# Row maxima between expert matmuls: listed places and a seventh bank, an output addition on two other engines, and an earlier overflow loop

## Chip, core and metric

The kernel runs on one core of a Trainium2 chip. Its engines work side by side: TensorE (PE in the profile; its weight loads are PEld), VectorE (DVE), ScalarE (ACT), GpSimd (POOL) and SyncE (SP, which issues most DMAs). The metric is the time of one execution in device microseconds.

## The reference, cut to what matters

```python
x = A_x                                             # 1 x 2048 x 448
g = sigmoid((x * gate_w).sum(-1, keepdims=True))
# A: full attention, 16 heads of 28
q, k, v = split_heads(x @ wqkv)
p = softmax(q @ k.T * 28 ** -0.5)
a = merge_heads(p @ v) @ wo
# B: mixture of 8 experts, each token goes to its top 2
logits = x @ w_gate
gates = softmax(top2(logits))
for e in range(8):
    h = silu(x @ w1[e]) @ w2[e]                     # 448 -> 1792 -> 448
    b += (gate of e for this token, else 0) * h
out = g * a + (1 - g) * b
```

All inputs are float32.

## The kernel before

There are three stages. The first (to about 134 us in the profiled execution) makes v, the gate and expert logits, the routing, and the queries and keys, which it stores in DRAM as a high and a low half. The second (134 to 957 us) computes the experts, each on its own gathered rows. The third is the attention: scores, exponential, values, projection, and the sum with the experts' rows.

The softmax of the attention needs, for each query and head, the maximum of its scores before the third stage starts. These maxima are computed in the second stage, between the experts' matmuls, from the high halves alone. `max_stream` is a generator over 1024 cells: group of four heads `g`, query tile `qt` of 128, key block `kc` of 512, head `j` in the group. A cell is one matmul with 28 rows (line 101); the four heads of a group lie on four row groups of the array. One step takes six cells into the six banks of the PSUM tile `pm`, and one VectorE instruction reduces the six (line 116). After the 16 cells of a query tile a small reduction folds them into `mg` (line 123), and after four query tiles `store_max` transposes `mg` on TensorE (line 133) into a new `pm` tile, copies it (line 135) and stores it in `m_d` (line 136). `pm` has one buffer of six banks; the two other banks of the eight are the accumulators `acc0` and `acc1`, which the experts use in turn.

An expert has two halves of seven hidden tiles (`NH`). In a half the first layer comes first: for each hidden tile two column halves of 288 tokens, 11 matmuls each (line 797), since inputs and weights are split in a high and a low part. ScalarE makes the hidden activations, GpSimd their low parts. Then the second layer takes five token tiles in the order 4, 0, 1, 2, 3: the tail tile 4 of 64 tokens (line 835) and four tiles of 128 tokens with 21 matmuls each (line 841). In the first half ScalarE copies the sums to `ysb` (line 849); in the second half VectorE adds `ysb` to the accumulator (line 859) and SP stores the sum in `ys_d` (line 861). In the second half of all experts but the last, `turn_x` also transposes the next expert's rows in the tiles, into the accumulator that is idle (line 696), and ScalarE copies them out twice (lines 699 and 700).

Where a step of the maxima goes is set by a running count. `worked(ns)` is called after every matmul of the experts with its assumed time, and once 3350 ns are owed, the next step of `max_stream` is issued:

```python
MAX_EVERY, STORE_NS = 3350, 1000
U_NS, Y_NS, YT_NS = 131, 206, 452
def worked(ns, fit=True):
    owed[0] += ns
    if fit and owed[0] >= MAX_EVERY:
        owed[0] = MAX_EVERY - STORE_NS if next(ms, 1) == 2 else 0
```

In a second half `fit` holds only for the first four matmuls of a token tile. The order on TensorE, VectorE, ScalarE and GpSimd is the order of the program; SP's issues are placed by the scheduler.

Tokens beyond 576 per expert go to overflow tiles, which `spilled` computes in a loop with a number of turns known only at run time (line 730; its inner loop goes over pairs of hidden tiles). It stands in the last token tile of the last expert, behind the fifth hidden tile; what is left of the maxima is issued right before it (`maxes(1 << 20)`).

Of the kernel before, what the change touches and what calls it, by code (L numbers as in the profile page):

```python
# [8 lines left out]
F32 = mybir.dt.float32  # L9
# [3 lines left out]
AF = mybir.ActivationFunctionType  # L13
ALU = mybir.AluOpType
AX = mybir.AxisListType
# [6 lines left out]
MAX_EVERY, STORE_NS = 3350, 1000  # L22
U_NS, Y_NS, YT_NS = 131, 206, 452
# [12 lines left out]
NF = FF // 128  # L36
# [13 lines left out]
def tile_gated_mha_moe(ctx: ExitStack, tc: tile.TileContext, x, wqkv, wo, wgate, w1, w2, gw, out):  # L50
# [38 lines left out]

    def max_stream():  # L90
        cells = [(g, qt, kc, j) for g in range(NG) for qt in range(NT) for kc in range(4) for j in range(4)]
        kh = {(0, c): load_khg(0, c) for c in range(4)}
        qgs = {(0, 0): load_qg(0, 0)}
        mgs, mps = {}, {}
        yield 0
        for b in range(0, len(cells), 6):
            step = cells[b:b + 6]
            pm = pmx.tile([128, 6, 512], F32, name="pm")
            for n, (g, qt, kc, j) in enumerate(step):
                rw = slice(32 * j, 32 * j + DH)  # L100
                nc.tensor.matmul(pm[:, n], qgs[g, qt // 4][rw, (qt % 4) * 128:(qt % 4 + 1) * 128],  # L101
                                 kh[g, kc][rw], start=True, stop=True)
# [10 lines left out]
            if b // 48 not in mps:  # L113
                mps[b // 48] = mxp.tile([128, 48], F32, name="mp")
            o = b % 48
            nc.vector.tensor_reduce(mps[b // 48][:, o:o + len(step)], pm[:, 0:len(step)], axis=AX.X, op=ALU.max)  # L116
            for n, (g, qt, kc, j) in enumerate(step):
                if kc == 3 and j == 3:
                    if qt % 4 == 0:
                        mgs[g, qt // 4] = mxp.tile([128, 4, 4], F32, name="mg")  # L120
                    mg = mgs[g, qt // 4]
                    part = mps[b // 48][:, o + n - 15:o + n + 1].rearrange("p (k j) -> p j k", j=4)
# [3 lines left out]
            yield 1  # L126
            if flush:
                store_max(*flush.pop())
                yield 2

    def store_max(g, qc, mg):
        pmt = pmx.tile([128, 6, 512], F32, name="pm")
        nc.tensor.transpose(pmt[0:16, 0, 0:128], mg.rearrange("p j t -> p (j t)"), ident)
        mr = mxp.tile([16, 128], F32R, name="mr")
        nc.vector.tensor_copy(mr, pmt[0:16, 0, 0:128])
        nc.sync.dma_start(m_d[4 * g + qc].rearrange("h (t q) -> (h t) q", q=128), mr.bitcast(F32))
        done.append((g, qc))

    flush = []
    done = []  # L140
    ms = max_stream()

    def maxes(n):
        for _ in range(n):
            next(ms, None)

    def need_max(g, qc):
        while (g, qc) not in done:
            next(ms, None)
# [18 lines left out]
    owed = [0]  # L168
# [53 lines left out]
    with ExitStack() as pa:  # L222
# [365 lines left out]
        maxes(1)  # L588
# [60 lines left out]
    with ExitStack() as pb:  # L649
# [39 lines left out]

        xf = sb.tile([128, 4, 512], F32, name="xf", bufs=1)  # L690
# [35 lines left out]
        def spilled():  # L726
# [3 lines left out]
            with tc.For_i(0, n_spill, 1) as it:  # L730
# [15 lines left out]
                with tc.For_i(0, NF // 2, 1) as c:  # L746
                    w1t_ = pe.tile([128, 4, 256], F32, name="w1r", bufs=3)
                    cs = ds(c * 256, 256)
                    nc.sync.dma_start(w1t_[:, 0:3], w1f[ds(ev * D, 384), cs].rearrange("(b p) n -> p b n", p=128))
                    nc.sync.dma_start(w1t_[0:64, 3], w1f[ds(ev * D + 384, 64), cs])  # L750
                    pu = pmx.tile([128, 6, 512], F32, name="pm")
                    for f in range(2):
                        w2t_ = sb.tile([128, D], F32, name="w2r", bufs=9)
                        nc.sync.dma_start(w2t_, w2f[ds(ev * FF + c * 256 + f * 128, 128)])
                        for b in range(4):
                            kk = 128 if b < 3 else 64
                            nc.tensor.matmul(pu[:, f, 0:128], w1t_[:kk, b, f * 128:(f + 1) * 128], xT[:kk, b],
                                             start=b == 0, stop=b == 3)
                        hT = sb.tile([128, 512], F32, name="hf32", bufs=3)[:, 0:128]
                        nc.scalar.activation(hT, pu[:, f, 0:128], AF.Silu)  # L760
                        nc.tensor.matmul(pu[:, 2, 0:D], hT, w2t_, start=f == 0, stop=f == 1)
                    nc.vector.tensor_tensor(yo, pu[:, 2, 0:D], yo, op=ALU.add)
                nc.sync.dma_start(ys_d[ds(it * 128 + NMAIN, 128)], yo)

        for e in range(E):
# [6 lines left out]
            for hf in range(2):  # L772
                hs = []
                lag = None
                for f in range(NH):
# [17 lines left out]
                    for c in range(2):  # L793
                        cs = slice(c * HC, (c + 1) * HC)
                        pu = accumulator()
                        for i, (a, b) in enumerate(mms):
                            nc.tensor.matmul(pu[:, 0:HC], a, b[:, cs], start=i == 0, stop=i == len(mms) - 1)  # L797
                            worked(U_NS)
# [22 lines left out]
                for n_k, k in enumerate((4, 0, 1, 2, 3)):  # L821
# [4 lines left out]
                    i = 0  # L826
                    for f in range(NH):
                        hh, hl, ht = hs[f]
                        w2h, w2l, w2r = w2t[base + f]
                        if (e, hf, n_k, f) == (E - 1, 1, 4, NH // 2 + 1):  # L830
                            maxes(1 << 20)
                            spilled()
                        if k == 4:
                            for c in range(2):
                                nc.tensor.matmul(py[64 * c:64 * c + n, 0:w], ht, w2r[:, c * w:(c + 1) * w],
                                                 start=f == 0, stop=f == NH - 1)
                            worked(YT_NS, hf == 0 or f == 0)
                            fetch_w2(base + f + 9)
                            continue
                        for a, b in ((hh, w2h), (hh, w2l), (hl, w2h)):  # L840
                            nc.tensor.matmul(py[:n, 0:w], a[:, cs], b, start=i == 0, stop=i == 3 * NH - 1)  # L841
                            i += 1
                            worked(Y_NS, hf == 0 or i < 5)
# [12 lines left out]
                    else:  # L856
                        r0 = e * CPAD + k * 128
                        yo = sb.tile([128, D], F32, name="yo")
                        nc.vector.tensor_tensor(yo[:, 0:w], py[:, 0:w], ysb[k][:, 0:w], op=ALU.add)
# [190 lines left out]
```

## Time and profile before

| | |
|---|---|
| time, median of 3 runs | 1495.57 us (1494.75 to 1496.4) |
| time of the profiled execution | 1493.23 us |
| its span in the profile | 1491.4 us |
| TensorE busy | 1473.6 us, 99% |
| VectorE, ScalarE, GpSimd busy | 806.7, 882.3, 613.8 us |
| expert stage | about 134 to 957 us |
| attention, without the projection | about 957 to 1445 us |

A row of the timeline gives start, duration, engine, line, operation, the tile written and the tiles read, and in brackets the idle time before it with what ended it. A stage row gives for each engine its busy time (and instructions), then the granted TensorE clock as a share of full speed, the DMA share and GB/s. A row of the table of waits gives the total, how often, and the longest. Queues carry a q (PEldq, SPq).

### The profile page before, as it was taken

To read this page: it belongs to the slowest core of one execution; us is meant where nothing else is said; L and a number is where in the kernel's file an instruction comes from. 1 tells how busy PE (TensorE), PEld (TensorE's weight loads), DVE (VectorE), ACT (ScalarE), POOL (GpSimd) and SP (SyncE) were. 2 spreads that over 40 slices of the span, in tenths; PEclk is the share of its full clock that TensorE was granted. 3 is DMA by queue.
4 is the path that set the end of the run, shared out by engine and by line. 5 is a ranking of instruction groups with operands and counts; after the bars stand their busy time and mean duration, and the time that the engine had idled before them with its cause. 6 is when DMAs were issued, how large, how long until landed. Compare 5 with 4: busy or idle time off the path is not lost. (4 is left out here: it accounts for less than half of the span.)

```text
span 1491.4 us, 28369 instructions
## 1 busy us (share of the span) xinstructions
PE 1473.6 (99%) x11380; PEld 984.5 (66%) x11380; DVE 806.7 (54%) x672; ACT 882.3 (59%) x1539; POOL 613.8 (41%) x667
## 2 busy tenths in 40 slices
PE   8999999999999999999999999899999999999998
PEld 7878788788888887887888888533333333333348
DVE  4644777777768777767777777311122111123245
ACT  5324354344334433543443344399999999999981
POOL 2123575476457546754764565111113111214330
PEclk9999999999999999999999999999999999999999
DMA  9777631343233143313422410300221121143212
GB/s 322 259 250 233 177 96 55 106 123 96 76 120 114 42 124 120 96 54 107 126 84 73 120 60 1 92 21 21 68 66 52 54 66 34 29 112 107 71 37 103
DMA packets 107958, 147.97 MB, mean 99 GB/s; under 512 B 17356, under 2 KB 83308, under 8 KB 107824
## 3 DMA queue, kind: packets, MB, share of 16 engines
q1 hardware_dynamic: 98192, 124.90, 27.0%
q0 software_dynamic: 9344, 20.78, 4.8%
q8 instruction: 90, 1.47, 0.4%
q10 hardware_dynamic: 288, 0.46, 0.1%
q14 instruction: 44, 0.36, 0.1%
HBM read 108.56 MB, written 37.51 MB: 98 GB/s over the span
## 5 line engine op out<-in xcount | busy, mean ns | idle before, releaser
L116 DVE TENSOR_REDUCE mp<-pm 128x6 f32<-128x3072 f32 x171 | 573.1, 3351 | 141.7 <-PE pm L101 141.2
L966 ACT ACTIVATE P<-ps 128x1536 f32<-128x1536 f32 x256 | 370.7, 1448 | 0.0
L975 PE MATMUL po<-P,V 128*32 128x512 f32 x2048 | 273.7, 606 | 0.0
L797 PE MATMUL acc<-xeh,w1l 128*128 128x288 f32 x880 | 258.2, 300 | 0.0
L797 PE MATMUL acc<-xeh,w1h 128*128 128x288 f32 x880 | 257.3, 299 | 0.0
L714 POOL TENSOR_TENSOR w2l<-w2r,w2h 128x448 fp32r<-128x448 f32 x112 | 128.9, 1151 | 235.8 <-ACT w2h L708 204.9
L963 PEld LDWEIGHTS ps<-Q,Kh 29*128 29x128 f32 (+1 forms) x2048 | 79.4, 184 | 216.2 <-ACT P L965 215.7
L799 ACT ACTIVATE hh<-acc 128x288 fp32r<-128x288 f32 x224 | 92.1, 411 | 178.4 <-PE acc L797 178.4
L797 PE MATMUL acc<-xel,w1h 128*128 128x288 f32 x660 | 197.1, 299 | 0.0
L963 PE MATMUL ps<-Q,Kh 29*128 29x512 f32 (+1 forms) x2048 | 192.6, 446 | 1.6 <-ACT P L965 1.5
L930 POOL DMA_DIRECT2D sum_d<-osb x64 | 31.9, 509 | 353.6 <-DVE osb L979 353.6
L797 PEld LDWEIGHTS acc<-xeh,w1l 128*128 128x128 f32 x880 | 166.1, 189 | 14.4 <-issue 14.2
L841 PE MATMUL acc<-w2h,hh 128*128 128x448 f32 x448 | 171.4, 383 | 2.3 <-DMA Kh<-neg_d 2.3
L797 PEld LDWEIGHTS acc<-xeh,w1h 128*128 128x128 f32 x880 | 165.9, 189 | 11.2 <-issue 11.0
L841 PE MATMUL acc<-w2l,hh 128*128 128x448 f32 x448 | 169.3, 378 | 0.0
L841 PE MATMUL acc<-w2h,hl 128*128 128x448 f32 x448 | 165.9, 370 | 0.0
L979 DVE COPY osb<-po 128x512 f32<-128x512 f32 x16 | 11.1, 691 | 283.2 <-PE po L975 283.2
L965 ACT ACTIVATE P<-ps 128x512 f32<-128x512 f32 x256 | 153.0, 598 | 7.0 <-PE ps L963 6.2
L679 POOL TENSOR_TENSOR w1l<-w1r,w1h 128x512 fp32r<-128x512 f32 (+1 forms) x88 | 137.8, 1566 | 19.2 <-ACT w1h L673 6.9
L723 POOL TENSOR_TENSOR hl<-hf,hh 128x512 fp32r<-128x512 f32 x112 | 143.2, 1286 | 0.0
L797 PEld LDWEIGHTS acc<-xel,w1h 128*128 128x128 f32 x660 | 124.7, 189 | 7.9 <-issue 7.7
L101 PE MATMUL pm<-khg,qg 28*128 28x512 f32 x1024 | 124.9, 460 | 1.1 <-DVE mp L116 1.0
(179 smaller groups left out, 1855.3 us busy)
## 6 DMA issues: line engine op xcount, KB each, us to landing
w2r<-in_B_w_dram SPq DMA_DIRECT2D x112, 224.0 KB
w1r<-in_B_w_dram SPq DMA_DIRECT2D x56, 384.0 KB
w1r<-in_B_w_dram SPq DMA_DIRECT2D x112, 64.0 KB
qkh_d<-hi SPq DMA_DIRECT2D x28, 256.0 KB
qkl_d<-lo SPq DMA_DIRECT2D x28, 256.0 KB
ys_d<-yo SPq DMA_DIRECT2D x32, 224.0 KB
ys_d<-zf SPq DMA_DIRECT2D x24, 224.0 KB
v_d<-v_s SPq DMA_DIRECT2D x16, 256.0 KB
```

What stands on the lines that cost most here:

```text
L101: nc.tensor.matmul(pm[:, n], qgs[g, qt // 4][rw, (qt % 4) * 128:(qt % 4 + 1) * 128], kh[g, kc][rw], start=True, stop=True)
L116: nc.vector.tensor_reduce(mps[b // 48][:, o:o + len(step)], pm[:, 0:len(step)], axis=AX.X, op=ALU.max)
L679: nc.gpsimd.tensor_tensor(l[:, :, half], r[:, :, half], h[:, :, half].bitcast(F32), op=ALU.subtract)
L714: nc.gpsimd.tensor_tensor(w2l, w2r, w2h.bitcast(F32), op=ALU.subtract)
L723: nc.gpsimd.tensor_tensor(hl, hf32, hh[:, 0:512].bitcast(F32), op=ALU.subtract)
L797: nc.tensor.matmul(pu[:, 0:HC], a, b[:, cs], start=i == 0, stop=i == len(mms) - 1)
L799: nc.scalar.activation(hh[:, cs], pu[:, 0:HC], AF.Silu)
L841: nc.tensor.matmul(py[:n, 0:w], a[:, cs], b, start=i == 0, stop=i == 3 * NH - 1)
L963: nc.tensor.matmul(p3[:, j - 1] if j else p1, k[rw, ks], qs[u][rw, c], start=i == 0, stop=i == 2)
L965: nc.scalar.activation(P[:, 0], p1, AF.Exp, scale=SCALE)
L966: nc.scalar.activation(P[:, 1:4], p3, AF.Exp, scale=SCALE)
L975: nc.tensor.matmul(po[32 * j:32 * j + 32], v[:, kt % 8, 32 * j:32 * j + 32], P[:, j], start=kt == 0, stop=kt == NT - 1)
```

## The change

- The planner's count is gone. `w1_due` lists the places in a half's first layer where a step goes: five, or six in the second halves of the last four experts (`six`). In the second layer one step goes to the start of the tail tile (with `six`: behind its fourth hidden tile) and one to each of the four other token tiles, at the fifth or the twelfth matmul (`free_at`).
- In those four tiles a step takes seven cells: the first goes to the bank of the accumulator that is idle just then (`other_accumulator`), and has a reduction of its own; the six others go to `pm` as before. Exceptions are the second half's first tile of 128 tokens where it transposes in two places (`two`).
- `store_max` no longer takes a `pm` tile: it transposes into the idle accumulator's bank, at such a place, in a step's stead; the step follows `STORE_NS` = 600 ns later. The maxima lie in one ring of 256 columns.
- The second half's sum is made by a ScalarE copy out of the accumulator and a GpSimd addition, no longer by VectorE.
- The loop over overflow tokens stands in the tile before the last, behind its third hidden tile, and its inner loop takes one hidden tile a turn instead of two. All maxima have been issued by then.

The diff, cut:

```diff
-MAX_EVERY, STORE_NS = 3350, 1000
+STORE_NS = 600
...
-        for b in range(0, len(cells), 6):
-            step = cells[b:b + 6]
+        mp = mxp.tile([128, 256], F32, name="mp", bufs=1)
+        while b < len(cells):
+            more = len(spare)
+            step = cells[b:b + 6 + more]
             pm = pmx.tile([128, 6, 512], F32, name="pm")
+            banks = spare[:] + [pm[:, n] for n in range(len(step) - more)]
...
-                nc.tensor.matmul(pm[:, n], qgs[g, qt // 4][rw, ...],
+                nc.tensor.matmul(banks[n], qgs[g, qt // 4][rw, ...],
                                  kh[g, kc][rw], start=True, stop=True)
...
+            if more:
+                nc.vector.tensor_reduce(mp[:, o:o + 1], banks[0], axis=AX.X, op=ALU.max)
...
-    def store_max(g, qc, mg):
-        pmt = pmx.tile([128, 6, 512], F32, name="pm")
-        nc.tensor.transpose(pmt[0:16, 0, 0:128], mg.rearrange("p j t -> p (j t)"), ident)
+    def store_max(g, qc, mg, bank):
+        nc.tensor.transpose(bank[0:16, 0:128], mg.rearrange("p j t -> p (j t)"), ident)
...
-    def worked(ns, fit=True):
-        owed[0] += ns
-        if fit and owed[0] >= MAX_EVERY:
-            owed[0] = MAX_EVERY - STORE_NS if next(ms, 1) == 2 else 0
+    def worked(ns, due=False, bank=None):
+        hold[0] = max(0, hold[0] - ns)
+        want[0] += due
+        if want[0] and not hold[0]:
+            if flush and bank:
+                store_max(*flush.pop(0), bank())
+                hold[0] = STORE_NS
+                return
+            if bank:
+                spare.append(bank())
+            next(ms, None)
+            want[0] -= 1
+            spare.clear()
...
+        def other_accumulator():
+            return ps.tile([128, 512], F32, name=f"acc{turn[0] ^ 1}")
...
-                with tc.For_i(0, NF // 2, 1) as c:
+                with tc.For_i(0, NF, 1) as f:
...
+        NM = 11
+        w1_due = [(18, 46, 73, 100, 128), (7, 33, 59, 85, 111, 137)]
...
+                six = hf == 1 and e >= E - 4
...
-                            worked(U_NS)
+                            worked(U_NS, 2 * NM * f + c * NM + i in w1_due[six])
...
+                    turns = hf == 1 and e + 1 < E
+                    two = turns and n_k == 1
+                    free_at = 12 if n_k == 1 and six or turns and not two else 5
+                    if k == 4:
+                        worked(0, not six)
...
-                        if (e, hf, n_k, f) == (E - 1, 1, 4, NH // 2 + 1):
-                            maxes(1 << 20)
+                        if (e, hf, n_k, f) == (E - 1, 1, 3, 3):
+                            assert not flush and next(ms, 0) == 0
                             spilled()
...
-                            worked(YT_NS, hf == 0 or f == 0)
+                            worked(YT_NS, six and f == 3)
...
-                            worked(Y_NS, hf == 0 or i < 5)
+                            worked(Y_NS, i == free_at, other_accumulator if free_at <= i < 17 and not two else None)
...
-                        nc.vector.tensor_tensor(yo[:, 0:w], py[:, 0:w], ysb[k][:, 0:w], op=ALU.add)
+                        nc.scalar.activation(yo[:, 0:w], py[:, 0:w], AF.Copy)
+                        nc.gpsimd.tensor_tensor(yo[:, 0:w], yo[:, 0:w], ysb[k][:, 0:w], op=ALU.add)
```

More of the change, by code (lines that the diff above doesn't have):

```diff
@@ L140, in tile_gated_mha_moe @@
     done = []
+    spare = []
     ms = max_stream()
-    def maxes(n):
-        for _ in range(n):
-            next(ms, None)
     def need_max(g, qc):
-        while (g, qc) not in done:
-            next(ms, None)
+        assert (g, qc) in done
     def tail_twice(xt):
@@ L586, in first_x @@
                 x_tile(xgs[k], k, lambda: ps.tile([128, 4, 128], F32, name="pt"), *xe)
-        maxes(1)
+        next(ms)
         xgs = [gather(0, k) for k in range(5)]
```

59 lines of the change are left out of this document (30 added, 29 removed).

## The prediction

> **What bounds the kernel now.** I read the page's first part, then the busy times by stage, then who waited for whom, and last the rows of TensorE in order of time. The first fence is the page (busy time; two groups: count, busy us, mean ns, idle before), then one stretch of the expert stage, then two rows of the table of waits.
>
> ```profile
> PE 1473.6 (99%) x11380; PEld 984.5 (66%) x11380; DVE 806.7 (54%) x672; ACT 882.3 (59%) x1539; POOL 613.8 (41%) x667
> L116 DVE TENSOR_REDUCE mp<-pm 128x6 f32<-128x3072 f32 x171 | 573.1, 3351 | 141.7 <-PE pm L101 141.2
> L101 PE MATMUL pm<-khg,qg 28*128 28x512 f32 x1024 | 124.9, 460 | 1.1 <-DVE mp L116 1.0
> ```
> ```profile
> 200.00:300.00 100.00, 99.74 (x664) 81.60 (x663) 75.33 (x36) 40.74 (x111) 59.44 (x53) 1.00 0.31 95
> ```
> ```profile
> PE acc L841 <- DMA Kh<-neg_d: 2.3, 1, 2.3
> PE pm L101 <- DVE mp L116: 1.0, 4, 0.3
> ```
>
> TensorE is busy 99.74 of 100 us in the expert stage, ScalarE 40.74, GpSimd 59.44, VectorE 75.33. Nearly nothing holds TensorE up: four short waits for the maxima, and one of 2.3 us at the loop over overflow tokens. So the time of this stage is the number of TensorE instructions times what each costs, and only fewer or cheaper TensorE steps can shorten it. The max matmuls come as 171 bursts among the experts' matmuls. What is a burst worth? These are TensorE's rows in order of time (start, duration, instruction):
>
> ```profile
> 204.09 0.29 PE L797 MATMUL acc<-xel,w1h 128*128 128x288 f32 x1
> 204.22 0.29 PE L797 MATMUL acc<-xeh,w1l 128*128 128x288 f32 x1
> 204.44 0.73 PE L101 MATMUL pm<-khg,qg 28*128 28x512 f32 x6
> 205.11 0.40 PE L797 MATMUL acc<-xeh,w1h 128*128 128x288 f32 x1
> 205.34 0.30 PE L797 MATMUL acc<-xeh,w1l 128*128 128x288 f32 x1
> ...
> 943.04 0.37 PE L841 MATMUL acc<-w2h,hl 128*128 128x448 f32 x1
> 943.24 0.37 PE L841 MATMUL acc<-w2h,hh 128*128 128x448 f32 x1
> 943.54 0.51 PE L101 MATMUL pm<-khg,qg 28*128 28x512 f32 x4
> 943.98 0.47 PE L841 MATMUL acc<-w2l,hh 128*128 128x448 f32 x1
> ```
>
> Starts of neighbours, not durations, give the price, since matmuls overlap. A first-layer matmul follows the last after 0.13 us, a second-layer one after 0.20. Round the burst of six the starts go 204.22, 204.44, 205.11, 205.34: 1.12 us for two steps that take 0.26 without it. A burst of six costs **0.86 us**: 0.09 to get in, 0.67 inside, 0.10 to get going again. From first start to the next other matmul the burst of four takes 0.44, that of six 0.67: two more matmuls 0.22.
>
> **The change part by part.**
>
> *Fewer bursts.* In the order of the built program the changed kernel has 162 bursts for the same 1024 matmuls: 107 of six, 54 of seven, one of four. Nine bursts fewer at 0.86: **-7.7 us**. That holds if a seventh matmul is nearly free. Four row groups run side by side, and seven consecutive cells use each at most twice, as six do. How two full rounds go is seen in the attention stage, where eight matmuls of the same width stand in a row:
>
> ```profile
> 958.23 0.74 PE L963 MATMUL ps<-Q,Kh 29*128 29x512 f32 x8 [0.68 <-ACT P L965]
> 958.80 0.40 PE L963 MATMUL ps<-Q,Kl 28*128 28x512 f32 x4
> ```
>
> Two rounds of four take 0.57, so one takes 0.285. If neighbours in a round stand s apart, a burst of six ends 0.285 - 2s after one of four; that is 0.22, so s is 0.033, and the seventh costs 0.033 us. Bounds: nothing, and 0.11 (half of the 0.22 for two). I take 0.033, because the rows of full rounds lie nearest: 54 x 0.033 = **+1.8 us** (0 to 5.9).
>
> [...]
>
> *Listed places.* Bursts stood wherever the planner's 3350 ns were up. Where one came late in the first layer and the next right after the tail tile, TensorE waited for the reduction:
>
> ```profile
> 316.64 0.47 PE L841 MATMUL acc<-w2h,hh 128*128 128x448 f32 x1
> 317.37 0.73 PE L101 MATMUL pm<-khg,qg 28*128 28x512 f32 x6 [0.25 <-DVE mp L116]
> ```
>
> 0.73 to get in, not 0.30: 0.43 lost, four times by the table of waits. In the new list first-layer bursts stand 26 or 27 matmuls apart: 26 x 0.13 + 0.86 = 4.2 us, against a reduction of 3.35. Second-layer ones are a tile apart: 21 x 0.20 + 0.86 = 5.1, against 3.35 and a seventh of some 0.56 (a sixth of 3.35). So the four waits go: **-1.7 us** (0 to -1.7). One pair, in the last half of the last expert, is only 14 matmuls apart (3.7 us), which may give back 0.5; that lies within this bound.
>
> *The seventh's bank.* The burst now also waits for whoever read the idle accumulator last. In the tiles that also transpose the next expert's rows (three per second half of seven experts, 21 bursts) that is ScalarE's second copy, and the burst stands six matmuls behind the transposes:
>
> ```profile
> 215.78 0.60 PE L696 MATMUL acc<-ident,xg 128*128 128x128 f32 x4
> ```
> ```profile
> 216.42 0.60 ACT L699 ACTIVATE xeh<-acc 128x512 fp32r<-128x512 f32 x1 [3.80 <-PE acc L696]
> 216.91 0.59 ACT L700 ACTIVATE xf<-acc 128x512 f32<-128x512 f32 x1
> ```
>
> The copies end at 217.50, 1.72 us behind the transposes' start. TensorE gets there after four transposes (about 0.45 with the restart), six matmuls of 0.20 and 0.1 to get in: 1.75. That is a draw. I take 0.05 each: **+1.0 us** (0 to 12.6, the latter if one more ScalarE instruction of 0.60 stands ahead). The other 33 sevenths use a bank that a copy at the start of the tile frees within 0.8 us, and stand at five matmuls (1.0 us) or later: nothing.
>
> *Stores of maxima.* The transposes go from the six-bank tile to the idle accumulator.
>
> ```profile
> 285.73 0.37 PE L841 MATMUL acc<-w2h,hl 128*128 128x448 f32 x1
> 286.21 0.27 PE L133 MATMUL pm<-ident,mg 128*16 128x128 f32 x1
> 286.24 0.45 PE L841 MATMUL acc<-w2h,hh 128*128 128x448 f32 x1
> ```
>
> The most one costs is 286.24 - 285.73 - 0.20 = 0.31 us. Sixteen remain, and ten again carry a separate semaphore instruction in front, as ten do before: no change (-2 to +2).
>
> *The output's addition* goes from VectorE to a copy on ScalarE and an addition on GpSimd (groups by line):
>
> ```profile
> L714 POOL TENSOR_TENSOR w2l<-w2r,w2h 128x448 fp32r<-128x448 f32 x112 | 128.9, 1151 | 235.8 <-ACT w2h L708 204.9
> L849 ACT ACTIVATE ysb<-acc 128x448 f32<-128x448 f32 (+1 forms) x40 | 20.3, 507 | 161.5 <-PE acc L841 138.7 <-PE acc L835 22.8
> ```
>
> 40 x 0.51 = 20 us more on ScalarE and 40 x 1.15 = 46 us more on GpSimd, which stood idle 235.8 us ahead of those very splits. The addition frees no accumulator, so TensorE waits for the copy alone, which lasts no longer than VectorE's addition: nothing, as long as GpSimd's transposed inputs are ready when the next expert starts. On SP the stores of the output leave some 1.1 us later; loads of weights and of keys queue behind them, but are fetched a pair of columns or a query block ahead.
>
> *The loop.* The trace shows no instruction of its body: it turns zero times, and the one-tile body costs nothing here. But every engine walks through its entry and exit, where it waits for all work and all DMAs ahead. Rows round it, from TensorE, VectorE, SP, the branch line and ScalarE:
>
> ```profile
> 948.14 0.36 PE L841 MATMUL acc<-w2h,hh 128*128 128x448 f32 x1
> 950.49 0.37 PE L841 MATMUL acc<-w2h,hl 128*128 128x448 f32 x1
> 953.17 0.47 PE L841 MATMUL acc<-w2h,hh 128*128 128x448 f32 x1 [2.31 <-DMA Kh<-neg_d]
> 955.39 0.58 PE L841 MATMUL acc<-w2h,hl 128*128 128x448 f32 x1
> ```
> ```profile
> 948.39 0.62 DVE L859 TENSOR_TENSOR yo<-acc,ysb 128x448 f32<-128x448 f32 x1 [1.79 <-PE acc L841]
> ```
> ```profile
> 949.05 0.33 SPq L861 DMA_DIRECT2D ys_d<-yo  x1
> 949.50 0.35 SPq L136 DMA_DIRECT2D m_d<-mr  x1
> ```
> ```profile
> L730 PEldq EVENT_SEMAPHORE  x14: 51/51/51, 950.9 to 952.8; - x14
> ```
> ```profile
> 951.88 1.28 ACT L965 ACT_TABLE_LOAD   x1 [21.98 <-DMA m_d<-mr]
> 957.58 0.60 ACT L965 ACTIVATE P<-ps 128x512 f32<-128x512 f32 x1 [4.41 <-PE ps L963]
> ```
> ```profile
> 954.00:956.00 2.00, 2.00 (x11) 1.33 (x9) 0.00 (x0) 0.00 (x0) 0.34 (x1) 0.59 0.00 1
> 956.00:958.00 2.00, 1.55 (x12) 0.73 (x12) 0.62 (x1) 0.42 (x1) 2.00 (x5) 0.56 0.24 75
> 962.00:964.00 2.00, 2.00 (x16) 0.84 (x12) 0.00 (x0) 1.18 (x1) 0.98 (x1) 0.50 1.00 226
> ```
>
> The stall is 953.17 - 950.49 - 0.20 = 2.48 us. Count from the last matmul of the tile before it (948.14): the output's store leaves SP at +0.91, that of the maxima at +1.36, ScalarE is let go at +3.74, TensorE at +5.03. Moved to the fourth tile's ninth matmul, the same chain runs over the new route: copy from +0.25, 0.51, addition 1.15, so the output's store leaves at about +2.0, 1.1 later, the maxima's behind it, and TensorE is let go at +6.1 at the latest. It gets there at +2.1 (nine matmuls and a store). The stall is at most 6.1 - 2.1 - 0.2 = 3.8, and no less than 2.48, TensorE's own walk through fourteen semaphore instructions. I take 3.4, near the later end, because only part of that walk can be made while the DMAs are awaited: +0.9.
>
> Behind the stall the granted clock is 0.59 and 0.56: 0.41 x 2 + 0.44 x 2 = 1.7 us of full speed lost. Before, part of that falls on the first scores, ahead of ScalarE's first exponential; in the change 33 matmuls follow and all of it falls on them: +0.5. [...] ScalarE's table load, which lies inside the stall before, now comes behind the last copy: 0.25 + 0.51 + 1.28 = 2.0 us from the last matmul to the first exponential, as before (957.58 - 955.39 = 2.19): nothing. The loop in all: **+1.4 us** (0 to 3.0: 1.3 of stall, 1.7 of clock).
>
> **Sum:** -7.7 + 1.8 - 1.7 + 1.0 + 1.4 = -5.2 us. The profiled execution took 1493.23 (span 1491.4), which would become 1488.0; it lies 2.3 below the median of the runs, 1495.57, from which I carry the difference: **1490.4 us**. What a measurement can tell from no change is about 0.2%, 3 us: 1492.6 and 1498.6 are the borders.
>
> **The rivals.**
> *Everything hidden.* The seventh is free, no bank is waited for, the loop costs what it did, and the slow clock of 962 to 964 stays away since the attention starts warm: -7.7 - 1.7 - 1 = -10.4, 1485.2. For it: rounds are only half full. Against it: TensorE idles at the attention's start as before.
> *Cells, not bursts, are the price.* The seventh costs 0.11 (+5.9) and the loop its upper bound (+3.0): -7.7 + 5.9 - 1.7 + 1.0 + 3.0 = +0.5, 1496.1. For it: four to six costs 0.22. Against it: the attention's rounds.
> *ScalarE late at the bank (slower).* In the 21 tiles the copy of the output, new on ScalarE, stands ahead of the two copies of the transposes. If it waits (its buffer is one of two, each held until addition and store are through), all behind it waits, and TensorE with it: at 0.60 each 12.6 in place of 1.0, so +6.4, 1502. It decides once copy, addition, store and landing take longer than two tiles, 10 us; I count about 5.
> *GpSimd becomes the bound.* The last low halves of the next expert's inputs come late at seven starts; with 1 us each +7 - 5.2, 1497.4. By my count about 2 us of room are left there.
> That the change isn't what it says, I exclude for the bursts: 162 are in the program.
>
> **How the numbers follow.** The forecast has 0.54 (own range 1487 to 1493.5, of which 0.03 lies within 0.2%), everything hidden 0.18, cells 0.14, ScalarE late 0.09, GpSimd 0.05 (0.03 within, 0.02 above). Faster: 0.51 + 0.18 = 0.69; within 0.2%: 0.03 + 0.14 + 0.03 = 0.20; slower: 0.09 + 0.02 = 0.11. The range goes from 1485 (everything hidden) to 1497 (cells, and part of GpSimd's), leaving out ScalarE late and the tails.
>
> **What would show it.** In the profile after: 162 bursts; from first start to the next other matmul 0.70 for seven and 0.67 for six; no wait of TensorE for VectorE's maxima but one; TensorE's stall at the loop 2.5 to 3.8 us with a granted clock near 0.6 behind it; waits for ScalarE at the bursts under 2 us in all. Wrong it is if sevens take 0.78 or more, if those waits pass 8 us, or if a new wait stands at the experts' starts.

## The result and the profile after

| | before | after |
|---|---|---|
| time, median of 6 runs | 1495.06 us (1494.1 to 1496.4) | 1485.84 us (1484.16 to 1487.46) |
| ratio after to before, 95% interval | | 0.9941 (0.9930 to 0.9951) |
| profiled execution, its span | 1493.23, 1491.4 us | 1484.16, 1482.4 us |
| expert stage, start of its first to start of its last expert matmul | 133.96 to 955.39, 821.43 us | 132.30 to 946.26, 813.96 us |

The change made the kernel 9.2 us faster; forecast were 5.2. On another chip the changed kernel came to 0.9940 (0.9929 to 0.9952) of the kernel before. The numbers of the profile after, in the order in which those of before were read: first the page's busy times and VectorE's group of the maxima (count, busy us, mean ns, idle before), then the same stretch of the expert stage as before.

```profile
PE 1460.7 (99%) x11380; PEld 980.4 (66%) x11380; DVE 786.5 (53%) x680; ACT 902.9 (61%) x1579; POOL 657.5 (44%) x707
L125 DVE TENSOR_REDUCE mp<-pm 128x6 f32<-128x3072 f32 (+1 forms) x164 | 542.0, 3306 | 121.3 <-PE pm L106 121.3
```
```profile
200.00:300.00 100.00, 100.00 (x678) 82.96 (x677) 72.65 (x38) 45.40 (x120) 66.72 (x60) 1.00 0.31 96
```

The reductions count 164 where the bursts are 162, because the ring of 256 columns cuts two of them. TensorE does not rest at all in this stretch (100.00 us of 100). ScalarE and GpSimd are busier than before (45.40 for 40.74, 66.72 for 59.44), as the addition's move says. TensorE's table of waits holds three rows that matter, and that of its weight loads (PEld) one:

```profile
PE acc L868 <- DMA Kh<-qkh_d: 4.9, 1, 4.9
PE ps L991 <- ACT P L993: 3.6, 5, 1.6
PE pm L106 <- DVE mp L125: 0.4, 1, 0.4
```
```profile
PEld acc L141 <- ACT xf L718: 2.3, 7, 0.3
```

Of the four waits for VectorE's maxima one is left, the pair in the last half that the prediction named. No matmul of a burst waits for ScalarE, so the seventh's bank is free in time. The stores of the maxima (line 141), which now go to the same bank, are not so lucky: at seven of the sixteen the weight load waits until ScalarE's second copy has left the accumulator. These seven lengthen the spacing of the matmuls round them by 0.23 us, the other nine by 0.11; that is 0.9 us in all. The wait at the loop has doubled. A burst of six and a burst of seven, in order of time:

```profile
211.56 0.73 PE L106 MATMUL pm<-khg,qg 28*128 28x512 f32 x6
212.22 0.47 PE L868 MATMUL acc<-w2h,hl 128*128 128x448 f32 x1
...
220.50 0.49 PE L106 MATMUL acc<-khg,qg 28*128 28x512 f32 x1
220.50 0.73 PE L106 MATMUL pm<-khg,qg 28*128 28x512 f32 x6
221.16 0.47 PE L868 MATMUL acc<-w2h,hh 128*128 128x448 f32 x1
```

From the first start to the next expert matmul both take 0.66 us. Over all bursts it is 0.661 for six and 0.667 for seven: inside a burst the seventh matmul costs 0.006.

Now the loop, from GpSimd, SP and TensorE (SPq rows are the issues of DMAs), and below it TensorE's sequencer at the loop's branch line: the count of its semaphore instructions with the first and last start, and the same from 936.2 on.

```profile
931.30 1.15 POOL L887 TENSOR_TENSOR yo<-yo,ysb 128x448 f32<-128x448 f32 x1 [4.65 <-ACT yo L886]
932.15 0.37 PE L868 MATMUL acc<-w2h,hl 128*128 128x448 f32 x1
932.47 0.34 SPq L889 DMA_DIRECT2D ys_d<-yo  x1
932.94 0.35 SPq L144 DMA_DIRECT2D m_d<-mr  x1
937.46 0.74 PE L868 MATMUL acc<-w2h,hh 128*128 128x448 f32 x1 [4.95 <-DMA Kh<-qkh_d]
```
```profile
L748 PEldq EVENT_SEMAPHORE  x14: 51/51/51, 932.6 to 937.1; - x14
L748 PEldq EVENT_SEMAPHORE  x8: 51/51/51, 936.3 to 937.1; - x8
```

TensorE's last matmul ahead of the loop starts at 932.15, the next at 937.46. That is a stall of 937.46 - 932.15 - 0.20 = 5.11 us, against 2.48 before and 3.4 forecast (bound 3.8). The sequencer makes six of its fourteen steps, the sixth at 934.5, and then stands until 936.3; all five engines go on there, in the same 0.05 us. So they wait for something common. The waits' table blames the loads of the keys, but these leave SP at 936.93, after the release: the name is wrong. The two stores ahead of the loop fit better, and they leave SP only when GpSimd's addition is over at 932.45.

Behind the stall the granted clock (the third number from the right) is half:

```profile
936.00:938.00 2.00, 0.54 (x1) 0.50 (x2) 0.00 (x0) 0.00 (x0) 0.00 (x0) 0.50 0.08 16
938.00:940.00 2.00, 2.00 (x7) 1.78 (x6) 0.00 (x0) 0.00 (x0) 0.00 (x0) 0.50 0.33 105
940.00:942.00 2.00, 2.00 (x7) 1.78 (x6) 0.00 (x0) 0.00 (x0) 0.00 (x0) 0.50 0.00 0
942.00:944.00 2.00, 2.00 (x11) 1.78 (x11) 0.00 (x0) 0.55 (x1) 1.05 (x1) 0.97 0.00 0
```

Twelve matmuls stand 0.373 us apart there instead of 0.203: 2.0 us. The expert stage is 7.47 us shorter although its loop costs some 4 more (2.63 of stall, 1.4 of clock). Outside it, the first stage ended 1.66 us sooner, though no edit touches it, and the attention took as long as before.

### The profile page after: what moved, and what is told of

Its sections match the earlier page's. It is cut to its first block, busy times and chain, and to the rows that moved or that the text cites. A ratio compares the mean times of both kernels' runs of the same rounds, so it can differ in the third digit from the quotient of the medians.

```text
span 1482.4 us, 28384 instructions
## 1 busy us (share of the span) xinstructions
PE 1460.7 (99%) x11380; PEld 980.4 (66%) x11380; DVE 786.5 (53%) x680; ACT 902.9 (61%) x1579; POOL 657.5 (44%) x707
## 4 chain that ended last, share of the span: by engine, by line
PE 95%; issue 1%; DVE 1%; ACT 1%; DMA 1%; POOL 0%; SPq 0%; POOLq 0%; ACTq 0%
PE acc L818 23%; PE acc L868 19%; PE po L1003 17%; PE ps L991 16%; PE pm L106 6%; PE pq L572 4%; PE acc L862 3%; PE pq L369 2%; PE ps L949 2%; PE acc L106 2%; PE acc L714 1%; PE po L949 1%; PE pt L331 0%; DMA wv_r<-in_gate_w_dram 0%; DVE ot L499 0%
## 5 line engine op out<-in xcount | busy, mean ns | idle before, releaser
L125 DVE TENSOR_REDUCE mp<-pm 128x6 f32<-128x3072 f32 (+1 forms) x164 | 542.0, 3306 | 121.3 <-PE pm L106 121.3
L868 PE MATMUL acc<-w2h,hl 128*128 128x448 f32 x448 | 169.1, 378 | 0.0
L868 PE MATMUL acc<-w2l,hh 128*128 128x448 f32 x448 | 164.4, 367 | 0.0
L106 PE MATMUL pm<-khg,qg 28*128 28x512 f32 x969 | 118.2, 454 | 0.4 <-DVE mp L125 0.4
```

The lines of the kernel that those rows point to most:

```text
L106: nc.tensor.matmul(banks[n], qgs[g, qt // 4][rw, (qt % 4) * 128:(qt % 4 + 1) * 128], kh[g, kc][rw], start=True, stop=True)
L125: nc.vector.tensor_reduce(mp[:, (o + lo) % 256:(o + lo) % 256 + hi - lo], pm[:, lo:hi], axis=AX.X, op=ALU.max)
```

## The experiments

Two things were open: what holds all engines at the loop, and which of the small terms (seventh, stores, addition, burst) the prediction had wrong. Theory A for the loop: GpSimd is late, because it runs a semaphore instruction of 1.13 us (INC_SWDGE_SEM) in the path that skips the loop, after its addition. Theory B: the stores are late, that of the maxima last, and every engine waits until they have landed.

### The loop's place and the last addition

```diff
 # a_lastadd_dve: as the changed kernel, but in the last expert
+if e == E - 1:
+    nc.vector.tensor_tensor(yo[:, 0:w], py[:, 0:w], ysb[k][:, 0:w], op=ALU.add)
+else: ... (ScalarE copy, GpSimd addition)
 # a_loop_old: as the changed kernel, but
-if (e, hf, n_k, f) == (E - 1, 1, 3, 3):
+if (e, hf, n_k, f) == (E - 1, 1, 4, 4):
 # a_loop_old_lastadd: both
 # b_loop_new: as the kernel before, but
-if (e, hf, n_k, f) == (E - 1, 1, 4, NH // 2 + 1):
+if (e, hf, n_k, f) == (E - 1, 1, 3, 3):
```

The last expert's addition on VectorE:

> The changed kernel, with the output's addition of the last expert alone back on VectorE. In the changed kernel TensorE stands 5.1 us at the loop (932.15 to 937.46) and every engine passes the last exit event at 936.30. Theory A (GpSimd late: it reaches the loop 1.7 us later because of its addition, so the 1.13 us semaphore instruction in its skipped path, and what waits for that count, come late): GpSimd is through early, the stall falls to 2.5 to 3.0 us, the time by 2 to 2.6 us below the changed kernel's 1485.8, to about 1483.5. Theory B (the maxima's store, issued at 932.94, lands 3.0 to 3.4 us later and holds all): SP issues it at most 0.9 us sooner, since the output's store ahead of it no longer waits for GpSimd; stall 4.2 to 5.1 us, time 1485 to 1486.

The loop in its old place:

> The changed kernel with the loop alone back in its old place (last token tile, behind twelve matmuls); the addition stays on ScalarE and GpSimd. Theory A (GpSimd late): its addition ends 1.9 us after the tile's last matmul, its count follows 1.1 later and takes effect some 4 us after it began, so TensorE is let go 6.3 us after that matmul, where it has arrived at 2.4: stall 3.7 to 4.1 us. Theory B (the maxima's store): the last such store is a whole tile, 4.3 us, further ahead and has landed; stall 2.3 to 2.9 us, TensorE's own walk. Time by A about 1485, by B about 1483.5 (changed kernel 1485.8); in both a second half-clock window may come back in the attention, +1.5.

Both:

> The changed kernel with the loop in its old place and the last expert's addition on VectorE: neither GpSimd nor the maxima's store can be late. A and B: stall 2.3 to 2.6 us, as before the change. Time 1483 to 1484; if the half clock behind the loop meets the attention's start and costs a second window, 1485. If the stall stays above 3.5 us, both theories fall.

The loop alone moved, in the kernel before:

> The kernel before, with the loop alone in its new place (tile before the last, behind nine matmuls); what is left of the maxima is issued right before it, the additions are all on VectorE. Theory A (GpSimd late): GpSimd has nothing to do there; stall 2.3 to 2.9 us, time as before (1495.1) to +0.6. Theory B (the maxima's store): the last maxima are stored right at the loop; the store lands 3 us after its issue, which is about 1 us after TensorE's arrival: stall 4 to 5 us, time +1.5 to +3.

| kernel | time, us | ratio to before | stall at the loop, us |
|---|---|---|---|
| a_lastadd_dve | 1482.41 (1480.38 to 1483.48) | 0.9903 (0.9886 to 0.9919) | 2.5 |
| a_loop_old | 1484.23 (1482.36 to 1484.43) | 0.9919 (0.9906 to 0.9932) | 2.65 |
| a_loop_old_lastadd | 1484.1 (1480.13 to 1485.62) | 0.9916 (0.9901 to 0.9931) | 2.5 |
| b_loop_new | 1495.34 (1494.43 to 1497.2) | 0.9998 (0.9989 to 1.0006) | 2.9 |

The kernel before was at 1496.09 on this chip. The stalls are from start to start, less one matmul of 0.20.

a_lastadd_dve came out at A's figure (2.5 to 3.0) and not at B's (4.2 to 5.1). It moves both suspects, though: GpSimd has no addition there, and the stores leave SP at 933.68 and 934.42, up to TensorE's last matmul ahead of the loop (934.52), where in the changed kernel they leave 0.3 and 0.8 us behind it. B was right on the 0.9 us sooner and wrong that this would save so little. a_loop_old_lastadd came out as expected.

The old place decides against A. GpSimd has its addition right ahead of the loop there too, and its semaphore instruction (INC_SWDGE_SEM) starts late. First its row in the changed kernel, then in a_loop_old, and there TensorE's wait:

```profile
L748 POOLq INC_SWDGE_SEM  x1: 1134/1134/1134, 932.1 to 932.1; - x1
```
```profile
L748 POOLq INC_SWDGE_SEM  x1: 1134/1134/1134, 936.5 to 936.5; - x1
```
```profile
PE acc L868 <- issue: 2.5, 1, 2.5
```

From that instruction to the release are 4.2 us in the changed kernel (932.1 to 936.3) and 2.4 in the old place (TensorE goes on at 938.9), and TensorE's row names no one at all. What differs is the store of the maxima: it is a tile further ahead in the old place. b_loop_new, meant to have that store late, does not test it: the scheduler put the store behind the loop on SP, which leaves the loop at 946.9 (its last branch) and issues the store at 947.05:

```profile
L730 SPq COMPARE_BRANCH  x1: 42/42/42, 946.9 to 946.9; - x1
```
```profile
947.05 0.33 SPq L136 DMA_DIRECT2D m_d<-mr  x1
```

It shows something else: the loop's move alone, with the last maxima right ahead of it, is worth nothing (0.9998).

With the additions of the last expert on VectorE the stall is gone as well, but a new wait of 1.5 us stands at the bursts, the price of VectorE's addition behind a reduction:

```profile
PE acc L106 <- DVE yo L887: 1.5, 2, 1.3
```

### What made the store so late

Three of the runs have the loop in the new place with GpSimd's addition ahead of it, and the same order round it: the changed kernel, a_store_pm and a_no_seventh (both described below). The last of them stalls only 3.55 us (936.99 - 933.24 - 0.20). The DMA view tells them apart. Its rows show a window in 40 slices: busy tenths of the DMA engines, then GB/s. First the changed kernel from 932.5 on over 4.5 us, then a_store_pm from 933.0 on over 4.2 us, in slices of 0.105:

```profile
DMA  0000200599897360001000000000000000000000
q1 hardware_dynamic: 176, 0.24, 14.7%
q8 instruction: 1, 0.02, 1.6%
```
```profile
DMA  0000300008998972900000010000000000000000
GB/s 0 0 0 0 78 0 0 0 17 324 358 375 307 427 273 83 239 10 0 0 0 0 0 78 0 5 0 0 0 0 0 0 0 0 0 0 0 0 0 0
q8 instruction: 1, 0.02, 1.4%
```

The 176 packets of q1 are the two stores. In a_store_pm 174 of them are through by 934.9 (the eighteenth slice), then nothing of them moves, and the last two packets (512 and 4 bytes) come alone, the 5 GB/s in slice 26 (935.65). In between q8 loads 16 KB of instructions in one packet: it is booked at 934.7 (in the 239 GB/s of slice 17) and takes 0.94 us of one DMA engine, as its share says (1.4% of 16 engines over 4.2 us). 934.7 + 0.94 is when the two late packets come. In the changed kernel the load is booked at 934.07 and takes 1.15 us, and the two late packets come at 935.2. The engines are let go 1.1 us later in both (936.3 and 936.7). And a_no_seventh, from 933.5 on over 3.1 us, with the release of TensorE's sequencer below it:

```profile
DMA  0000004000028999999624200000030000000000
q1 hardware_dynamic: 176, 0.24, 21.8%
q14 instruction: 2, 0.02, 1.9%
```
```profile
L747 PEldq EVENT_SEMAPHORE  x8: 51/51/51, 935.9 to 936.6; - x8
```

No q8 load, no late packets; the engines go on at 935.9, 1.9 us after the issue of the maxima's store (934.03) instead of 3.4. TensorE's stream is 55 matmuls and as many weight loads shorter there; whether that is why the load stays away was not shown. Nor was it seen directly that the load holds the two packets up, on a DMA engine that both share; shown is only that its end and their coming agree (935.64 and 935.65, 935.22 and 935.2).

What holds the engines in a_no_seventh, where nothing lands late? The rows of its loop line from 935.4 on (first and last start):

```profile
L747 SPq COMPARE_BRANCH  x2: 41/42/43, 935.6 to 936.6; - x2
L747 ACTq EVENT_SEMAPHORE  x9: 38/38/38, 935.7 to 936.4; - x9
L747 PEldq EVENT_SEMAPHORE  x9: 51/51/51, 935.7 to 936.6; - x9
```

Of SP's two branches in these rows the first is at 935.6, and all four other engines make their next step together 0.1 us later (COMPARE_BRANCH is a jump, EVENT_SEMAPHORE a step). In the changed kernel it is the same at 934.3 and 934.5 (TensorE's sixth step), in a_store_pm at 935.15 and 935.27. So the engines first wait for SP, which comes to the loop late because it issues the two stores before. In a_no_seventh that is all: behind 935.9 no engine stands any more. Where a load came between, all five engines stand a second time, until after the store's last packets (935.2 and 936.3, 935.65 and 936.7). The changed kernel was run once more, on another chip:

> The changed kernel once more, on the same chip as the version with one addition on VectorE. Theory (stores late): stall at the loop 3.4 us if no instruction load shares a DMA engine with the maxima's store, 4.7 to 5.1 if one does; the semaphore event that lets all engines go comes 0.5 to 1.1 us after the last packet of that store in either case. Rival (GpSimd's semaphore instruction): the event has a fixed distance from that instruction, whatever the packets do. Time 0.994 of the kernel before.

The load is booked at 935.7 and takes 0.99 us, the last two packets come at 936.69 and 936.75, and the release is at 937.75, with a stall of 938.85 - 933.82 - 0.20 = 4.83 us. From GpSimd's semaphore instruction (933.8) to the release it is 3.95 us here, 2.7 in a_no_seventh, 4.0 in a_store_pm and 4.2 in the first profile: no fixed distance. From the end of the store's last packet to the release it is about 1.0 us in all three profiles with the load (in a_no_seventh at most 0.6; why less is open). Theory A has fallen. Of B this is left: the late stores hold all engines, first because SP issues them before it comes to the loop, and then, with the load, until about 1.0 us behind the last packet.

### Seventh, stores, addition, burst

```diff
 # a_no_seventh: as the changed kernel, the seventh cell left out
-for n, (g, qt, kc, j) in enumerate(step):          # matmuls
+for n, (g, qt, kc, j) in list(enumerate(step))[more:]:
-if more:
-    nc.vector.tensor_reduce(mp[:, o:o + 1], banks[0], axis=AX.X, op=ALU.max)
 # b_36_fewer: as the kernel before, every fourth burst left out (matmuls, reduction)
+left = (b // 6) % 4 == 2 and 8 <= b // 6 < 152
 # a_store_pm: as the changed kernel, in store_max
+bank = pmx.tile([128, 6, 512], F32, name="pm")[:, 0]
 # a_add_dve: as the changed kernel, for all experts
+nc.vector.tensor_tensor(yo[:, 0:w], py[:, 0:w], ysb[k][:, 0:w], op=ALU.add)
-nc.scalar.activation(yo[:, 0:w], py[:, 0:w], AF.Copy)
-nc.gpsimd.tensor_tensor(yo[:, 0:w], yo[:, 0:w], ysb[k][:, 0:w], op=ALU.add)
```

> The changed kernel in which the 54 seventh cells are left out (neither matmul nor reduction; their maxima are missing), the bursts and places stay. If a seventh is free, as the starts in the trace of the changed kernel say (0.66 us from the first start to the next other matmul for seven as for six), the time stays at 1485.8 within the noise of about 0.7. At the prediction's 0.033 us each it falls by 1.8, at the rival's 0.11 (cells are the price) by 5.9 to 1480.

It came to 1484.46 us, 0.9930 (0.9915 to 0.9944) of before (1494.32 on this chip; the changed kernel has 0.9941). The expert stage is 1.54 us shorter than in the changed kernel, and its stall at the loop 1.56 (3.55 for 5.11). But the clock is half for sixteen matmuls behind it and not for twelve, which takes 4 x 0.17 = 0.7 us back, so about 0.7 is left for the sevenths, 0.7 / 54 = 0.013 us each: more than the starts say, under the forecast 0.033 and far under 0.11. (With the 54 the first cell of the burst of four was left out.)

> The kernel before with 36 of its 171 bursts of six left out (every fourth of the eighth to the 151st; their maxima are missing). At the prediction's price of 0.86 us a burst, and the four waits for VectorE gone as well: 36 x 0.86 = 31.0, with the waits 32.5, so 1495.5 less that, 1463 to 1464.5. If only the inside counts (0.67 each), 24 less, 1471. [...]

1465.13 us, 0.9800 (0.9786 to 0.9815): 29.9 us for 36 bursts, **0.83 us each** (0.77 to 0.89). In the trace the expert stage lasts 791.65 us, 29.78 less. The prediction's 0.86 was 4% too high; the inside alone, 0.67, is out.

> The changed kernel with the stores' transposes back in the six-bank tile, at the same places. If the bank of the store matters as the traces suggest (a store costs some 0.13 us less in the idle accumulator's bank), the time rises by about 2, to 1488, and by a little more if the burst behind a store waits for VectorE's copy out of the six-bank tile. By the prediction (nothing) it stays at 1485.8.

1485.27 us, 0.9937 (0.9922 to 0.9951), the same as the changed kernel. In the traces a store lengthens the spacing of the matmuls round it by 0.11 us here, by 0.16 in the changed kernel and by 0.28 in the kernel before (all 16 in the mean). My expectation was wrong: what is saved, 16 x 0.12 = 1.9 us, comes from the places of the stores, not from their bank. The idle accumulator even costs the 0.9 us of the seven waits for ScalarE, which are gone here: all sixteen take 0.11. In the kernel before nine stores stand 0.1 us behind a semaphore instruction of TensorE and cost 0.36 to 0.45 each, the seven others 0.12 to 0.19; at the new places these instructions come 0.3 us ahead or more.

> The changed kernel with the output's addition back on VectorE for all experts. The prediction gave this part nothing. If so, only the loop's stall is spared, as with the last expert's addition alone on VectorE: 1482.5. The other theory: on VectorE the addition stands behind a burst's reduction, so the accumulator's bank, which the seventh needs, comes free late; with the last expert alone TensorE waited 1.5 us at two bursts for it. Over eight experts that is 8 to 12 us, less the 3 of the loop: 1490 to 1495.

1516.11 us, 1.0160 (1.0138 to 1.0183): 30 us slower than the changed kernel, far beyond either theory. The table of waits says where:

```profile
PE acc L714 <- DVE yo L886: 25.2, 18, 2.4
PE acc L818 <- DVE yo L886: 7.0, 7, 1.5
```

VectorE is the one waited for: with bursts in the middle of a tile it is still reducing when the tile ends, so its addition comes late and the accumulator stays taken. In the kernel before, with the bursts of these second halves at the start of the tiles, the same addition has no such row. Hardly any burst waits for that (a single 1.3), but 18 times the transposes of the next expert's rows (line 714) do, 25.2 us, and seven times the first layer. The addition's move is therefore not idle: it is what the new places stand on.

### Versions without the late store

> The changed kernel with one addition, that of the last expert's third tile (the one whose store SP issues right ahead of the loop), on VectorE instead of ScalarE and GpSimd. Theory (stores late: the output's store waits for GpSimd's addition, the maxima's store queues behind it on SP, and every engine waits at the loop's exit until both have landed, with 1.1 to 1.3 us on top where an instruction load shares a DMA engine with them): both stores leave SP about 1 us sooner, ahead of the instruction load; stall 2.3 to 2.9 us in place of 5.1. With the last expert's additions all on VectorE TensorE waited 1.3 us at a burst for a bank; that is not so here. Time 1485.8 - 2.4 = 1483.4 or a little less. Rival (GpSimd's semaphore instruction holds the engines): GpSimd has no addition ahead of the loop either, the same stall; the two were told apart by the loop in its old place.

```diff
+if e == E - 1 and n_k == 2:
+    nc.vector.tensor_tensor(yo[:, 0:w], py[:, 0:w], ysb[k][:, 0:w], op=ALU.add)
```

The stall is 2.5 us (2.31 from the end of the last matmul), the time 1481.41 us, 0.9923 (0.9909 to 0.9936). On one chip with the changed kernel:

> The version with the one addition ahead of the loop on VectorE, on the same chip as the changed kernel: stall 2.3 us, and 2 to 3.5 us faster than the changed kernel, 0.992 of the kernel before. If the two agree within 0.7 us, the late stores are not what the time hangs on, and the stall is taken back elsewhere.

1483.34 us (1481.85 to 1484.99), 0.9930 (0.9917 to 0.9943), beside 1484.82 (1483.79 to 1487.13) and 0.9940 for the changed kernel. The stall fell by 2.4 us again, the median by 1.5, less than the 2 to 3.5 expected; with runs that spread over 3 us and intervals that overlap, that is not certain to be a gain. Two profiles of this one version show where part of it goes. The first is the profile on the first chip, the second that on the other; both stalls are 2.31:

```profile
935.00:938.00 3.00, 2.99 (x15) 2.79 (x16) 0.00 (x0) 0.26 (x1) 0.00 (x0) 1.00 0.31 78
...
946.00:950.00 4.00, 3.33 (x24) 1.04 (x20) 0.00 (x0) 3.52 (x4) 3.64 (x7) 0.50 0.98 206
```
```profile
934.60:938.00 3.40, 3.34 (x9) 3.00 (x10) 0.00 (x0) 0.00 (x0) 0.00 (x0) 0.50 0.25 69
...
946.00:950.00 4.00, 3.14 (x32) 0.90 (x24) 0.00 (x0) 4.00 (x5) 3.81 (x8) 0.78 0.81 226
```

After the same stall the clock is full in one and half in the other, and the first has it half in the attention's start instead. Last, the loop behind all expert matmuls:

> The changed kernel with the loop at the very end of the expert stage: behind the last expert's last matmul, ahead of the attention's first scores; the additions of the last two tiles on VectorE, so that ScalarE goes from the loop straight to its table load and the first exponential. Theory (the walk of 2.3 us, the clock halved behind it, 1.5 to 2 us, and the 2.2 us from the last expert matmul to the first exponential are three separate losses, and here they overlap): from the last expert matmul to the first exponential about 4 us, against 2.3 + 2.0 + 2.2 = 6.5 with the loop earlier and no late store, 9.3 in the changed kernel's trace. Time 1485.8 - 5 = 1481. Rival (the loads of the second half of the keys, which are issued behind the loop, come late, or the slow clock holds the first scores longer): 2 to 4 us lost again, 1483 to 1485.

```diff
-                        if (e, hf, n_k, f) == (E - 1, 1, 3, 3):
-                            ...
-                            spilled()
+                    if (e, hf, n_k) == (E - 1, 1, 4):
+                        spilled()
```

1480.87 us (1480.8 to 1482.45), 0.9919 (0.9906 to 0.9933). The last expert matmul starts at 940.44 and the first exponential at 944.68, 4.24 us, as expected; but the scores behind it run on half the clock for eight microseconds and more:

```profile
944.00:948.00 4.00, 2.65 (x24) 1.19 (x20) 0.00 (x0) 2.93 (x4) 3.62 (x7) 0.50 0.83 208
948.00:952.00 4.00, 4.00 (x28) 1.50 (x28) 0.00 (x0) 2.89 (x3) 0.98 (x1) 0.50 1.08 226
```

So the overlap was won, and part of it was lost to the clock. This version and a_add2_dve, on the same chip, differ by 0.5 us, within their spread. All versions without the late store lie at 0.990 to 0.993 and the two comparisons of the changed kernel at 0.994; which of them is best can't be said.

## Why the prediction was right, and where it was off

**The mechanism held.** Fewer bursts are the gain: nine of them at 0.83 measured, -7.4 us (forecast -7.7). Direction, range and the step "only fewer or cheaper TensorE steps shorten this stage" were right. The point was 4.6 us too high. In the profiles the expert stage gained 7.5 where the sum had 5.2, and that is two errors against each other, below; 1.7 more lies in the first stage, which is luck of the profiled execution and nothing that was forecast.

**Terms that were too dear.** The seventh: +1.8 forecast, 54 x 0.006 = +0.3 measured. By a_no_seventh it is about 0.7. The step that failed is the spacing of 0.033, taken from full rounds of the attention; the lower bound was nearer. The bank: +1.0 forecast for the bursts, and none waits; the draw with ScalarE's second copy was lost by seven stores instead, 0.9. Stores: 0 forecast, -1.9 measured, with these 0.9 already in it; that as many semaphore instructions cost as much as before is the step that failed. The waits for VectorE: -1.7 forecast; the one pair that is left gives 0.4 back, -1.3.

**The loop was too cheap.** +1.4 forecast, +4.0 in the profile, above its bound of 3.0. The chain itself was right: the output's store at +2.0 from the tile's last matmul (930.43 to 932.47), the maxima's behind it. Forecast was the last release "at the latest" at +6.1; it was at +7.0, because the bound assumed that a store lands as fast as before, and an instruction load of 1.15 us came between. Of "all work and all DMAs ahead" the runs show SP and the two stores, nothing beyond. Without the load, in a_no_seventh, the stall is 3.55, where the prediction said 3.4.

**The clock.** Two microseconds were lost behind the stall, forecast 1.7. All of it falls in the expert stage, where before only 0.6 did. In the attention's start, 962 to 964 had half the clock before, and after, the clock is 1.00 from 950 on; but in a_add2_dve it is 0.50 again there (946 to 950), so this was no effect of the change that can be counted on. The first stage gained 1.66 us that no edit explains. TensorE waits there for the same 2.3 us in both kernels, and then the clock is half in one and full in the other (before, then after):

```profile
80.00:82.00 2.00, 2.00 (x13) 1.33 (x13) 1.02 (x3) 0.60 (x1) 0.00 (x0) 0.63 0.98 371
82.00:84.00 2.00, 2.00 (x12) 1.81 (x12) 0.30 (x1) 0.00 (x0) 0.00 (x0) 0.51 1.00 381
```
```profile
80.00:82.00 2.00, 2.00 (x22) 1.64 (x22) 1.02 (x2) 0.60 (x1) 0.00 (x0) 1.00 1.00 371
82.00:84.00 2.00, 2.00 (x17) 1.52 (x15) 0.29 (x2) 0.60 (x1) 0.00 (x0) 1.00 1.03 381
```

That is not a gain of the change. The first stage is the same program in all runs, and it ends at 133.68 in the second profile of the changed kernel and at 132.38 in b_loop_new, where it is the kernel before's. How much of the 9.2 us between the medians is due to it can't be told.

**The sum for the expert stage**: bursts -7.4, sevenths +0.3, waits -1.3, stores -1.9, stall +2.6, clock +1.4, together -6.3, where 7.5 were measured. The 1.2 us left over stay open.

**The rivals.** "Everything hidden" (1485.2, chance 0.18) came nearest to the time and was right on the seventh and on the bank for the bursts, and wrong on the loop; that the slow clock of 962 to 964 stayed away was luck. "Cells are the price" fell with the 0.66 us of a burst of seven. "ScalarE late" shows in the 0.9 us of seven stores, and "GpSimd the bound" in no row of waits. What was missed is how close the other side lay: with the addition left on VectorE the same edits are 22 us slower than before.

**A slip in the description:** before the change the loop stood behind the fourth hidden tile of the last token tile (twelve matmuls), not the fifth; the numbers of the prediction are counted from the trace and do not depend on it.

## What to carry to other kernels

Price a burst of foreign matmuls by leaving some out (here 0.83 us for six), and fill it before you add another: the entry (0.09) and the exit (0.10) were paid already, and one more matmul cost 0.006 us by the starts, 0.013 by a_no_seventh. When a burst is moved into a stretch where it was not allowed, look for the work of the other engines that is released by the same tile end, and move that first (a_add_dve, where it stayed, was 30 us slower). And look at what is stored right ahead of a loop whose turns are known only at run time: here stores that left SP up to TensorE's last matmul ahead of it cost nothing, and a store that left 0.8 us later cost 1.1 us without an instruction load and 2.4 to 2.6 with one, because all engines waited at the loop for SP and, with the load, for the last packet.

## What the runs showed of the hardware

- A loop of zero turns cost TensorE 2.5 us in a_lastadd_dve and a_add2_again, where the last store left SP 0.1 us before TensorE's last matmul ahead of it started (934.42 and 934.52, 931.88 and 931.99).
- A load of 16 KB of instructions in one packet starts 1.1 to 1.2 us behind TensorE's second branch at the loop's line in the kernel before (952.27 behind 951.2), the changed kernel (934.07 behind 932.9) and a_store_pm (934.7 behind 933.5), and takes 0.94 to 1.15 us; in a_no_seventh none comes up to the release, so the branch alone does not settle it. Of a store that was still under way, the last packets came 0.8 to 1.1 us behind the others (changed kernel twice, a_store_pm).
- The clock does not follow the length of a stall alone: behind the same 2.31 us it was 1.00 in a_add2_dve (935 to 938) and 0.50 in a_add2_again (934.6 to 938). Why was not shown.
- The releaser that the table of waits names at such a loop can be wrong: in the changed kernel it named loads of the keys that SP issued at 936.93, after the release at 936.3.
